# Two inner-layer tiles of a fused attention + MLP kernel handled as one

## The chip, the core and the metric

The kernel runs on one core of a Trainium2 chip. The metric is the time of one execution on the device in microseconds (us); less is better. The engines are TensorE (PE in the profile; PEld is its weight load), VectorE (DVE), ScalarE (ACT), GpSimd (POOL) and the queue that issues the DMAs (SP). Each works through its own instructions in order and waits on semaphores for the others.

## The reference, cut to what matters

```
# attention over clusters: B=4, H=8, S=768, D=64, 16 clusters
mask   = (argmax(q_n @ c_n.T)[:, :, :, None] == argmax(k_n @ c_n.T)[:, :, None, :])
scores = where(mask, (q @ k.T) / sqrt(D), -1e9)
attn   = softmax(scores);  x = (attn @ v) as [3072, 512]
# MLP
h = x @ w_in                    # [3072, 2048]
g = s * relu(h) ** 2 + b
out = g @ w_out                 # [3072, 512]
```

## The kernel before

**Attention in units.** A unit is 128 queries of one head: 4 batches, 3 chunks of 256 tokens each, 4 head pairs, 2 query tiles, 2 heads, so 192 units. A unit takes its scores on TensorE (`scores`, 4 matmuls, L456), the row maximum on VectorE (`maxima`, L465), a tiny bias and the exponential on ScalarE (`exps`, L472 and L475), the f16 high part of the exponential on ScalarE (`high`, L119; on VectorE for some early units) and the low part on GpSimd (`low`, L498), a transposing DMA of both (L500), and the product with V on TensorE (`values`, L517 to L519, two units at a time). After 4 units `finish_x` splits the result into two f16 parts (L540 on ScalarE, L543 on GpSimd) and turns it by DMA into the tiles `x` that the MLP reads.

**MLP in steps.** A step is one chunk of 256 tokens and one of 16 blocks `ft` of 128 inner columns, so 12 chunks of 16 steps, 192 in all. Step by step: `mlp_in` multiplies by 12 matmuls of 128x256 (4 blocks of K, three f16 products each) into a tile `h` in PSUM; `mlp_relu` on ScalarE makes `r` from it (L582), then its square once in f16 as the high part `g[:, 0]` (L584) and once in f32 in place (L585); `mlp_gl` on GpSimd subtracts the one from the other as the low part (L590); `mlp_out` adds 6 matmuls of 128x512 into the two banks of `acc` (L602). After the last step of a chunk, VectorE scales `acc` into `o` (L610) and a DMA stores it. The pool of `h` has one buffer, so the next `mlp_in` waits until L582 has read the last one; `r` has 2 buffers and `g` 4.

**The order.** One loop over `i` writes everything: unit `i`, and MLP step `m = i - LAG` with `LAG = 21`. In turn it writes `scores(i)`, `mlp_out` of step `m-2`, `high(i-1)`, `maxima(i)` and `exps(i)`, `mlp_in` and `mlp_relu` of step `m`, `low(i-1)`, `mlp_gl` of step `m-1`, and in odd `i` `values(i-5)`. Preparations run beside it as generators, one piece in each turn: `prep_q`, and for the next batch `prep_k` and `prep_v`, which start 20 units ahead of it (mostly VectorE), and `wsplit(ft)`, which splits the weights of block `ft`. A scheduler then sets the real order on each engine by a simulation of its own, with what was written first preferred among what is ready; each engine's order is fixed when the kernel runs. A chunk's first step needs all four tiles `x` of its chunk, that is, all 16 of its units.

Of the kernel before, what the change touches and what calls it, by code (L numbers as in the profile page):

```python
# [8 lines left out]
F16 = mybir.dt.float16  # L9
# [9 lines left out]
P = 128  # L19
C = 16  # L20
D = 64
# [5 lines left out]
def tile_cluster_attention_mlp(ctx, tc, q, k, v, cent, w_in, w_out, s_in, b_in, out):  # L27
# [107 lines left out]

    ct = sb.tile([P, 2, D], F32, tag="r", name="ct", bufs=2)
    cn = ct[:, 0, :]
# [14 lines left out]

    cnat = sb.tile([P, 3, 2, D], F16, tag="r", name="cnat", bufs=2)
    G.memset(cnat[:, 1:3], 0.0)
# [402 lines left out]
    def mlp_start(b, c):  # L557
# [9 lines left out]
        MS[(b, c)] = [cf, xm[:, 7:8], None]  # L567

    def mlp_in(b, c, ft):
        n = f"{b}_{c}_{ft}"  # L570
        ph = ps_h.tile([P, 512], F32, tag="h", name=f"h_{n}")
        GS[(b, c, ft)] = ph
        terms = [(kt, wl, xl) for kt in range(KT) for wl, xl in ((0, 0), (0, 1), (1, 0))]
        for i, (kt, wl, xl) in enumerate(terms):
            nc.tensor.matmul(ph[:, :CW], WSP[ft][0][:, wl, kt, :], XS[(b, c, kt)][:, :, xl, :],  # L575
                             start=(i == 0), stop=(i == len(terms) - 1))

    def mlp_relu(b, c, ft):
        n = f"{b}_{c}_{ft}"
        ph = GS[(b, c, ft)]  # L580
        r = sb.tile([P, CW], F32, tag="r", name=f"r_{n}", bufs=2)
        A.activation(r, ph[:, :CW], AF.Relu, scale=MS[(b, c)][0])  # L582
        g = sb.tile([P, 2, CW], F16, tag="g", name=f"g_{n}", bufs=4)
        A.activation(g[:, 0, :], r, AF.Square)  # L584
        A.activation(r, r, AF.Square)  # L585
        GS[(b, c, ft)] = (r, g)

    def mlp_gl(b, c, ft):
        r, g = GS[(b, c, ft)]
        G.tensor_tensor(g[:, 1, :], r, g[:, 0, :], op=ALU.subtract)  # L590
        GS[(b, c, ft)] = g

    def mlp_out(b, c, ft):
        n = f"{b}_{c}"
        if ft == 0:
            MS[(b, c)][2] = ps_a.tile([P, CT, DM], F32, tag="acc", name=f"acc_{n}")
        acc = MS[(b, c)][2]
        g = GS.pop((b, c, ft))
        for t in range(CT):
            rows = slice(t * P, t * P + P)  # L600
            for gl, wl in ((0, 0), (0, 1), (1, 0)):
                nc.tensor.matmul(acc[:, t, :], g[:, gl, rows], WSP[ft][1][:, wl, :],  # L602
                                 start=(ft == 0 and gl + wl == 0), stop=(ft == NF - 1 and gl == 1))
        if ft == NF - 1:
            _, e, acc = MS.pop((b, c))
            o = sb.tile([P, CT, DM], F32, tag="stage", name=f"o_{n}", bufs=3)
            if b + c == 0:
                column_sums()
            for t in range(CT):
                V.scalar_tensor_tensor(o[:, t, :], acc[:, t, :], e, bias[0], op0=ALU.mult, op1=ALU.add)  # L610
            nc.sync.dma_start(out[b * S : (b + 1) * S].rearrange("(p t) e -> p t e", t=T)[:, c * CT : (c + 1) * CT, :], o)
# [7 lines left out]
    def at(step, gen):  # L619
        later.setdefault(step, []).append(gen)  # L620
# [18 lines left out]
    for ft in range(NF):  # L639
        at(LAG - 4 + ft, wsplit(ft))  # L640
    wgen = weights()
# [58 lines left out]
    while i < NU + 8 or i - LAG < NS + 4:  # L700
# [4 lines left out]
        if i < NU:  # L705
            with first_of_all(i):
                scores(i)
        if 0 <= m - 2 < NS:
            mlp_out(*steps[m - 2])
        if 0 <= i - 1 < NU:  # L710
            with first_of_all(i):
                high(i - 1)
        if i < NU:
            with first_of_all(i):
                maxima(i)
                exps(i)
        if 0 <= m < NS:
            if steps[m][2] == 0:
                mlp_start(*steps[m][:2])
            mlp_in(*steps[m])  # L720
            mlp_relu(*steps[m])
        if 0 <= i - 1 < NU:
            with first_of_all(i):
                low(i - 1)
        if 0 <= m - 1 < NS:
            mlp_gl(*steps[m - 1])
# [34 lines left out]
```

## Time and profile before

| | before |
|---|---|
| time, median of 3 runs | 984.87 us (982.25 to 988.37) |
| the profiled execution | 987.78 us |
| its span in the profile | 986.0 us |
| PE / DVE / ACT / POOL busy | 834.3 / 673.0 / 726.4 / 550.2 us |
| `h` matmuls (L575) | 2304, 292.0 us busy |
| `acc` matmuls (L602) | 1152, 295.4 us busy |

The profile is of one execution. A row of a group names the line, engine, operation, the tiles written and read with their shapes, the count, the busy time in us and the mean of one in ns, and then the time its engine sat idle just before, with what ended that. The ends of matmuls are modelled and overlap, so the busy times of single lines on PE add up to more than PE's own.

### The profile page before, as it was taken

What the parts mean: (1) busy time and instruction counts of PE and PEld (TensorE: products, weight loads), DVE (VectorE), ACT (ScalarE), POOL (GpSimd) and SP (SyncE); (2) the same over time, 40 slices, a digit from 0 to 9 for tenths busy, and PEclk for the clock granted to TensorE, in tenths of its full rate; (3) what the DMA queues carried; (4) which work ended last, traced back from release to release, by engine and by line L of the source; (5) the groups of instructions that cost most, each with busy time, mean ns of one, the idle gap of its engine ahead of it and who ended that gap; (6) DMA issues with size and microseconds to landing.
All of it is one profiled execution on the core that took longest, in us unless ns stands there. A gap on an engine that the chain in (4) does not pass through costs nothing. (4 is left out here: it accounts for less than half of the span.)

```text
span 986.0 us, 22497 instructions
## 1 busy us (share of the span) xinstructions
PE 834.3 (85%) x8625; PEld 580.2 (59%) x8625; DVE 673.0 (68%) x1475; ACT 726.4 (74%) x1416; POOL 550.2 (56%) x543
## 2 busy tenths in 40 slices
PE   0568524887899999998799999997889999999997
PEld 0347312654566666765566666765666666767764
DVE  7798889989687665658787756578867567473100
ACT  4476776877578788867678877876788977789443
POOL 3125755556456576655467656655566766667322
PEclk9955566999999999999999999999999999999999
DMA  6865883687678775698888767797888676777200
GB/s 181 204 196 158 222 210 90 138 194 134 128 144 163 156 161 123 140 210 154 171 164 156 169 132 156 138 203 181 138 160 173 151 119 142 142 138 149 44 23 21
DMA packets 450299, 147.36 MB, mean 149 GB/s; under 512 B 417936, under 2 KB 446608, under 8 KB 450192
## 3 DMA queue, kind: packets, MB, share of 16 engines
q1 hardware_dynamic: 450192, 145.93, 69.7%
q8 instruction: 67, 1.10, 0.5%
q14 instruction: 40, 0.33, 0.1%
HBM read 35.69 MB, written 6.29 MB: 43 GB/s over the span
## 5 line engine op out<-in xcount | busy, mean ns | idle before, releaser
L498 POOL TENSOR_TENSOR ph<-p,ph 128x768 f16<-128x768 f32 x184 | 308.6, 1677 | 170.7 <-ACT ph L119 135.8
L575 PE MATMUL h<-x,wis 128*128 128x256 f16 x2304 | 292.0, 275 | 17.3 <-ACT r L582 12.2
L602 PE MATMUL acc<-wos,g 128*128 128x512 f16 x1152 | 295.4, 380 | 4.7 <-POOL g L590 2.9
L575 PEld LDWEIGHTS <-wis 128*128 128x128 f16 x2304 | 223.1, 98 | 74.9 <-issue 16.6
L590 POOL TENSOR_TENSOR g<-r,g 128x256 f16<-128x256 f32 x192 | 133.3, 695 | 139.7 <-ACT r L585 129.8
L465 DVE TENSOR_REDUCE ssm<-sc 128x1 f32<-128x768 f32 x192 | 180.9, 950 | 16.2 <-PE sc L456 16.0
L475 ACT ACTIVATE p<-sc,ssm,qsm 128x768 f32<-128x768 f32 x192 | 188.1, 980 | 3.9 <-DMA PT<-ph 1.8
L602 PEld LDWEIGHTS <-g 128*128 128x128 f16 x1152 | 104.1, 98 | 88.2 <-POOL g L590 6.9
L119 ACT ACTIVATE ph<-p 128x768 f16<-128x768 f32 x174 | 144.8, 832 | 11.1 <-DMA PT<-ph 10.8
L472 ACT ACTIVATE ssm<-ssm,lift,qsm 128x1 f32<-128x1 f32 x192 | 73.4, 382 | 101.9 <-DVE ssm L465 101.4
L517 PE MATMUL px<-vh,PT 128*128 128x65 f16 x1104 | 119.9, 196 | 14.5 <-DVE ksm L98 5.2
L582 ACT ACTIVATE r<-h,cf 128x256 f32<-128x256 f32 x192 | 89.1, 464 | 55.0 <-PE h L575 50.8
L518 PE MATMUL px<-vl,PT 128*128 128x64 f16 x1104 | 119.9, 193 | 0.0
L519 PE MATMUL px<-vh,PT 128*128 128x65 f16 x1104 | 119.9, 194 | 0.0
L456 PE MATMUL sc<-KA,QA 128*128 128x384 f16 x384 | 101.1, 343 | 20.2 <-ACT p L475 16.9
L518 PEld LDWEIGHTS <-PT 128*128 128x128 f16 x1104 | 103.6, 100 | 21.2 <-issue 12.8
L517 PEld LDWEIGHTS <-PT 128*128 128x128 f16 x1104 | 103.9, 98 | 17.5 <-issue 9.1
L456 PE MATMUL sc<-KB,QB 128*128 128x384 f16 x384 | 100.2, 345 | 7.8 <-DMA QB<-qb 7.7
L519 PEld LDWEIGHTS <-PT 128*128 128x128 f16 x1104 | 103.6, 98 | 3.0
L584 ACT ACTIVATE g<-r 128x256 f16<-128x256 f32 x192 | 79.5, 414 | 3.8
L585 ACT ACTIVATE r<-r 128x256 f32<-128x256 f32 x192 | 79.1, 412 | 3.3
L525 DVE TENSOR_SCALAR ssm<-px 128x2 f32<-128x2 f32 x92 | 14.2, 155 | 88.3 <-PE px L519 88.2
(153 smaller groups left out, 1090.9 us busy)
## 6 DMA issues: line engine op xcount, KB each, us to landing
wst<-in_moe_w_in_dram SPq DMA_DIRECT2D x16, 512.0 KB, 4.5
wst<-in_moe_w_out_dram SPq DMA_DIRECT2D x16, 512.0 KB, 4.1
kn<-in_k_dram SPq DMA_DIRECT2D x16, 384.0 KB, 3.9
qn<-in_q_dram SPq DMA_DIRECT2D x24, 256.0 KB, 3.8
vn<-in_v_dram SPq DMA_DIRECT2D x16, 384.0 KB, 4.4
out_dram<-o SPq DMA_DIRECT2D x12, 512.0 KB, 3.2
PT<-ph SPq DMA_TRANSPOSE x184, 3.4
x<-xn SPq DMA_TRANSPOSE x48, 2.5
```

The lines of the kernel that those rows point to most:

```text
L119: A.activation(dst, src, AF.Copy)
L456: last_score[0] = nc.tensor.matmul(sc[:, e, :HALF], X[:, col, :], y[:, h * S + e * HALF : h * S + (e + 1) * HALF], start=st, stop=not st)
L465: last_max[0] = V.tensor_reduce(SM[i // 4][:, 0, j : j + 1], U[i]["sc"], axis=AX.XY, op=ALU.max, negate=True)
L475: last_exp[0] = A.activation(p.rearrange("p (a b) -> p a b", a=2), u["sc"], AF.Exp, bias=bi, scale=u["scale"], **total)
L498: G.tensor_tensor(u["ph"][:, 1, :], u["p"], u["ph"][:, 0, :], op=ALU.subtract)
L517: nc.tensor.matmul(o1, PT[:, kt, :], vh[:, h, kt, : D + 1], start=(kt == 0), stop=False)
L518: nc.tensor.matmul(o, PT[:, kt, :], vl[:, h, kt, :], start=False, stop=False)
L519: nc.tensor.matmul(o1, PT[:, T + kt, :], vh[:, h, kt, : D + 1], start=False, stop=(kt == T - 1))
L575: nc.tensor.matmul(ph[:, :CW], WSP[ft][0][:, wl, kt, :], XS[(b, c, kt)][:, :, xl, :], start=(i == 0), stop=(i == len(terms) - 1))
L582: A.activation(r, ph[:, :CW], AF.Relu, scale=MS[(b, c)][0])
L590: G.tensor_tensor(g[:, 1, :], r, g[:, 0, :], op=ALU.subtract)
L602: nc.tensor.matmul(acc[:, t, :], g[:, gl, rows], WSP[ft][1][:, wl, :], start=(ft == 0 and gl + wl == 0), stop=(ft == NF - 1 and gl == 1))
```

## The change

Two neighbouring steps become one pair. `h` now holds two tiles of 256 columns, one bank of PSUM in all; `r` and `g` are twice as wide and have half the buffers (1 and 2), so they take the same room. Each ScalarE and GpSimd pass goes over both tiles. The numbers of matmuls and their shapes stay. `mlp_in` of a pair is written in the turns with even `m`, its squares in the next turn after the exponential (`mlp_square`, a function of its own now), `mlp_gl` in that turn too, and `mlp_out` three turns after `mlp_in` where it was two. `wsplit` starts one turn sooner. Two small tiles of the prologue, `ct` and `cnat`, get other buffers.

```diff
-    ct = sb.tile([P, 2, D], F32, tag="r", name="ct", bufs=2)
+    ct = sb.tile([P, 2, D], F32, tag="r", name="ct", bufs=1)
-    cnat = sb.tile([P, 3, 2, D], F16, tag="r", name="cnat", bufs=2)
+    cnat = sb.tile([P, 3, 2, D], F16, tag="g", name="cnat", bufs=2)
...
-        ph = ps_h.tile([P, 512], F32, tag="h", name=f"h_{n}")
+        ph = ps_h.tile([P, 2, CW], F32, tag="h", name=f"h_{n}")
-        for i, (kt, wl, xl) in enumerate(terms):
-            nc.tensor.matmul(ph[:, :CW], WSP[ft][0][:, wl, kt, :], XS[(b, c, kt)][:, :, xl, :],
-                             start=(i == 0), stop=(i == len(terms) - 1))
+        for f in range(2):
+            for i, (kt, wl, xl) in enumerate(terms):
+                nc.tensor.matmul(ph[:, f, :], WSP[ft + f][0][:, wl, kt, :], XS[(b, c, kt)][:, :, xl, :],
+                                 start=(i == 0), stop=(i == len(terms) - 1))
...
-        r = sb.tile([P, CW], F32, tag="r", name=f"r_{n}", bufs=2)
-        A.activation(r, ph[:, :CW], AF.Relu, scale=MS[(b, c)][0])
-        g = sb.tile([P, 2, CW], F16, tag="g", name=f"g_{n}", bufs=4)
-        A.activation(g[:, 0, :], r, AF.Square)
+        r = sb.tile([P, 2, CW], F32, tag="r", name=f"r_{n}", bufs=1)
+        A.activation(r, ph, AF.Relu, scale=MS[(b, c)][0])
+        GS[(b, c, ft)] = r
+
+    def mlp_square(b, c, ft):
+        r = GS[(b, c, ft)]
+        g = sb.tile([P, 2, 2, CW], F16, tag="g", name=f"g_{b}_{c}_{ft}", bufs=2)
+        A.activation(g[:, 0], r, AF.Square)
         A.activation(r, r, AF.Square)
...
-        G.tensor_tensor(g[:, 1, :], r, g[:, 0, :], op=ALU.subtract)
+        G.tensor_tensor(g[:, 1], r, g[:, 0], op=ALU.subtract)
...
-        for t in range(CT):
+        for f in range(2):
+            for t in range(CT):
...
-        at(LAG - 4 + ft, wsplit(ft))
+        at(LAG - 5 + ft, wsplit(ft))
...
-        if 0 <= m - 2 < NS:
-            mlp_out(*steps[m - 2])
+        if m % 2 and 0 <= m - 3 < NS:
+            mlp_out(*steps[m - 3])
...
+        if m % 2 and 0 <= m - 1 < NS:
+            mlp_square(*steps[m - 1])
-        if 0 <= m < NS:
+        if m % 2 == 0 and 0 <= m < NS:
             if steps[m][2] == 0:
                 mlp_start(*steps[m][:2])
             mlp_in(*steps[m])
...
-        if 0 <= m - 1 < NS:
+        if m % 2 and 0 <= m - 1 < NS:
             mlp_gl(*steps[m - 1])
```

What the scheduler makes of it is shown at two places. In the names, `h_2_4` is chunk 2, block 4 (the batch is left out), and the last number is that of the buffer's allocation.

On ScalarE, in the middle of chunk 2 of the first batch, before:

```order
L582 ACTIVATE r_2_4_4481<-h_2_4_4468,cf_2_4200 128x256
L584 ACTIVATE g_2_4_4483<-r_2_4_4481 128x256
L119 ACTIVATE ph_4597<-p_4556 128x768
L585 ACTIVATE r_2_4_4481<-r_2_4_4481 128x256
L472 ACTIVATE ssm_4417<-ssm_4417,lift,qsm_0_1_3834 128x1
L475 ACTIVATE p_4601<-sc_4586,ssm_4417,qsm_0_1_3834 128x768
L472 ACTIVATE ssm_4681<-ssm_4681,lift,qsm_0_1_3834 128x1
L582 ACTIVATE r_2_5_4571<-h_2_5_4558,cf_2_4200 128x256
```

And now, the same place after the change (L584 is now the relu, L590 and L591 are the squares):

```order
L584 ACTIVATE r_2_4_4362<-h_2_4_4337,cf_2_4083 128x512
L590 ACTIVATE g_2_4_4441<-r_2_4_4362 128x512
L185 ACTIVATE qb_1_0_4415<-qn_1_0_4197,qsm_1_0_4280 128x4x64 x2
L119 ACTIVATE ph_4435<-p_4335 128x768
L591 ACTIVATE r_2_4_4362<-r_2_4_4362 128x512
L472 ACTIVATE ssm_4307<-ssm_4307,lift,qsm_0_1_3746 128x1
L475 ACTIVATE p_4439<-sc_4418,ssm_4307,qsm_0_1_3746 128x768
L119 ACTIVATE ph_4459<-p_4439 128x768
L472 ACTIVATE ssm_4307<-ssm_4307,lift,qsm_0_1_3746 128x1
L475 ACTIVATE p_4463<-sc_4454,ssm_4307,qsm_0_1_3746 128x768
L584 ACTIVATE r_2_6_4490<-h_2_6_4465,cf_2_4083 128x512
```

From one relu to the next there lay one exponential (L475) before, and two now; three passes serve two steps where six did.

On GpSimd, where chunk 1 ends and chunk 2 begins in the second batch (the preparation of the third batch is about over there), before:

```order
L590 TENSOR_TENSOR g_1_14_7612<-r_1_14_7610,g_1_14_7612 128x256
L498 TENSOR_TENSOR ph_7673<-p_7595,ph_7673 128x768
L590 TENSOR_TENSOR g_1_15_7695<-r_1_15_7693,g_1_15_7695 128x256
L498 TENSOR_TENSOR ph_7743<-p_7678,ph_7743 128x768
L498 TENSOR_TENSOR ph_7840<-p_7747,ph_7840 128x768
L590 TENSOR_TENSOR g_2_0_7772<-r_2_0_7770,g_2_0_7772 128x256
```

And now (L596 is the subtraction for the pair):

```order
L596 TENSOR_TENSOR g_1_14_7416<-r_1_14_7344,g_1_14_7416 128x512
L543 TENSOR_TENSOR xn_7134<-xs_6971,xn_7134 128x2x128
L498 TENSOR_TENSOR ph_7180<-p_7159,ph_7180 128x768
L498 TENSOR_TENSOR ph_7288<-p_7184,ph_7288 128x768
L375 COPY qa_0_1_7267<-qb_0_1_7268 128x8x64
L428 MEMSET vh_0_9726 128x12x2
L498 TENSOR_TENSOR ph_7313<-p_7292,ph_7313 128x768
L543 TENSOR_TENSOR xn_7389<-xs_7255,xn_7389 128x2x128
L498 TENSOR_TENSOR ph_7409<-p_7317,ph_7409 128x768
L498 TENSOR_TENSOR ph_7458<-p_7414,ph_7458 128x768
L498 TENSOR_TENSOR ph_7569<-p_7462,ph_7569 128x768
L596 TENSOR_TENSOR g_2_0_7575<-r_2_0_7497,g_2_0_7575 128x512
```

The low parts of units (L498) between the last pair of chunk 1 and the first of chunk 2 are 6 now; between two pairs elsewhere there are mostly 2. Before, there were 3 for the two steps from `g_1_14` to `g_2_0`. So in the stretch before this place the MLP stands up to 4 steps further ahead of the units than it did, and here 4 more units pass without an MLP step. The same happens at this place in the first and the third batch.

More of the change, by code (lines that the diff above doesn't have):

```diff
@@ L598, in mlp_out @@
         g = GS.pop((b, c, ft))
-        for t in range(CT):
[L600 to L604, printed above, removed]
+        for f in range(2):
+            for t in range(CT):
+                rows = slice(t * P, t * P + P)
+                for gl, wl in ((0, 0), (0, 1), (1, 0)):
+                    nc.tensor.matmul(acc[:, t, :], g[:, gl, f, rows], WSP[ft + f][1][:, wl, :],
+                                     start=(ft + f == 0 and gl + wl == 0), stop=(ft + f == NF - 1 and gl == 1))
+        if ft == NF - 2:
             _, e, acc = MS.pop((b, c))
```

## The prediction

> **What bounds the kernel now.** I read the page's first two parts, then the windows of 50 us, the waits of TensorE and the chain that ended last. First the page: busy time of the engines, and the 40 slices of PE with its granted clock.
>
> ```profile
> PE 834.3 (85%) x8625; PEld 580.2 (59%) x8625; DVE 673.0 (68%) x1475; ACT 726.4 (74%) x1416; POOL 550.2 (56%) x543
> PE   0568524887899999998799999997889999999997
> PEclk9955566999999999999999999999999999999999
> ```
>
> The 85% is an average over two stages: PE is patchy for a quarter of the span, at a lower clock, and at 9 tenths or more after that, with two dents. The windows show the stages (start and end, length, then busy us and instructions of PE, PEld, DVE, ACT and POOL, granted clock, DMA share, GB/s):
>
> ```profile
> 150.00:200.00 50.00, 34.72 (x397) 24.00 (x397) 46.40 (x107) 38.21 (x73) 28.97 (x23) 0.80 0.47 106
> 200.00:250.00 50.00, 39.10 (x386) 24.73 (x384) 45.54 (x96) 37.56 (x70) 30.05 (x25) 0.95 0.82 165
> 400.00:450.00 50.00, 47.08 (x535) 33.39 (x533) 31.51 (x75) 38.87 (x78) 29.35 (x28) 1.00 0.83 175
> 450.00:500.00 50.00, 42.50 (x474) 29.61 (x470) 39.66 (x100) 37.42 (x71) 27.36 (x28) 1.00 0.81 165
> 500.00:550.00 50.00, 47.24 (x556) 33.41 (x555) 39.31 (x83) 40.64 (x78) 32.16 (x32) 1.00 0.88 171
> 650.00:700.00 50.00, 42.88 (x487) 30.48 (x485) 41.89 (x100) 36.50 (x71) 27.60 (x27) 1.00 0.82 171
> 750.00:800.00 50.00, 49.34 (x545) 34.48 (x543) 31.63 (x74) 40.91 (x81) 31.40 (x30) 1.00 0.73 156
> ```
>
> Up to 250 us VectorE is the full engine (46.40 and 45.54 of 50). From then on TensorE is: 47 to 49 of 50, but only 42.50 and 42.88 where the next batch is prepared and VectorE has 40 to 42 of 50. ScalarE, which the change relieves most, never has over 41. The chain that ended last has TensorE's work end to end in such a stretch (start, us, group):
>
> ```profile
> 618.56 1.29 PE acc L602 x6
> 619.86 1.30 PE sc L456 x8
> 621.15 1.31 PE h L575 x12
> ```
>
> So a step costs PE 1.31 + 1.29 = 2.60 us, and a unit 1.30 / 2 = 0.65 for its scores and, by this group's row, 119.9 / 1104 x 6 = 0.65 for its product with V: 1.30 in all, and 3.90 for a unit and a step.
>
> ```profile
> L517 PE MATMUL px<-vh,PT 128*128 128x65 f16 x1104 | 119.9, 196 | 14.5 <-DVE ksm L98 5.2 <-DVE xs L529 4.6 <-DVE xm L98 3.9
> ```
>
> The change keeps all this work. It can win only what PE stands idle, and from 250 us to the end its waits say for whom (us in total, times, longest):
>
> ```profile
> PE h L575 <- ACT r L582: 12.2, 10, 3.1
> PE sc L456 <- ACT p L475: 6.0, 6, 1.8
> PE sc L456 <- DMA QB<-qb: 5.8, 7, 2.0
> PE px L517 <- DVE ksm L98: 3.7, 3, 1.7
> PE acc L602 <- POOL g L590: 2.4, 6, 0.6
> ```
>
> **The passes themselves: nothing directly.** The groups, with equal shapes together:
>
> ```profile
> L582 ACT ACTIVATE r<-h,cf 128x256 f32<-128x256 f32 x192 | 89.1, 464 | 55.0 <-PE h L575 50.8 <-DVE xm L565 1.9 <-POOL g L590 0.8
> L584 ACT ACTIVATE g<-r 128x256 f16<-128x256 f32 x192 | 79.5, 414 | 3.8
> L585 ACT ACTIVATE r<-r 128x256 f32<-128x256 f32 x192 | 79.1, 412 | 3.3
> L119 ACT ACTIVATE ph<-p 128x768 f16<-128x768 f32 x174 | 144.8, 832 | 11.1 <-DMA PT<-ph 10.8 <-POOL ph L498 0.2
> L475 ACT ACTIVATE p<-sc,ssm,qsm 128x768 f32<-128x768 f32 x192 | 188.1, 980 | 3.9 <-DMA PT<-ph 1.8 <-POOL ph L498 0.8
> L472 ACT ACTIVATE ssm<-ssm,lift,qsm 128x1 f32<-128x1 f32 x192 | 73.4, 382 | 101.9 <-DVE ssm L465 101.4
> L267 ACT ACTIVATE wos<-wo,glob 128x512 f16<-128x512 f32 x16 | 11.5, 718 | 7.3 <-DVE wis L269 5.7 <-DVE glob L258 1.5
> L498 POOL TENSOR_TENSOR ph<-p,ph 128x768 f16<-128x768 f32 x184 | 308.6, 1677 | 170.7 <-ACT ph L119 135.8 <-ACT p L475 6.7 <-DVE ph L121 6.3
> L590 POOL TENSOR_TENSOR g<-r,g 128x256 f16<-128x256 f32 x192 | 133.3, 695 | 139.7 <-ACT r L585 129.8 <-DMA PT<-ph 4.5 <-issue 3.8
> L223 POOL TENSOR_TENSOR wi<-wi,wsg 128x512 f32<-128x512 f32 x16 | 20.1, 1255 | 33.1 <-PE pw L221 16.9 <-ACT ssm L472 13.5 <-DVE xs L529 2.7
> ```
>
> ScalarE: from 256 to 768 elements a pass grows by (832 - 414) / 512 = 0.816 ns an element, so a square over 512 takes 414 + 209 = 623 ns and a relu 464 + 209 = 673 (a scaled pass of 512 takes 718: the upper bound). 192 x (464 + 414 + 412) = 247.7 us become 96 x (673 + 2 x 623) = 184: 63 us less. GpSimd: (1677 - 695) / 512 = 1.92 ns, so 1186 for 512 (1255 at most): 133.3 become 114 to 120. Both lie beside PE's work; alone they are worth nothing, and count only through waits.
>
> **The wait for `h`: -5.1 us.** `mlp_in` needs the one bank of `h` read. Now PE has the next `mlp_out` and a unit between two `mlp_in` (1.29 + 1.30 = 2.6 us of cover for a pass of 0.46); then an `mlp_out` of a pair and two units (2.58 + 2.60 = 5.2 for 0.67). It takes a ScalarE that is over 4 us late, and the longest wait now is 3.1. But where the 12.2 us lie matters:
>
> ```profile
> PE h L575 <- ACT r L582: 3.0, 1, 3.0
> PE h L575 <- ACT r L582: 4.1, 2, 3.1
> ```
>
> These are the waits within 450 to 500 and 650 to 700: 7.1 us in the dents. There PE waits for a slow attention whatever name the wait bears. I count 12.2 - 7.1 = 5.1 as gone (bounds 0 and 12.2).
>
> The Trainium skill, Perfetto Trace Analysis, section Matmuls, says that independent groups of matmuls should rotate through PSUM banks, so that one is emptied beside the next one's matmuls. It speaks against a pair in one bank. By it each pair would stop PE for its relu, 96 x 0.67 = 64 us more; the wait row speaks for the cover, since one bank served 192 tiles with 10 waits.
>
> **The second product a turn later: -1.8 us.** `acc<-g` waits 2.4 us now; a turn of 3.9 us more before it removes them, apart from the last one (start, us, group, idle before):
>
> ```profile
> 980.07 1.04 PE L602 MATMUL acc<-wos,g 128*128 128x512 f16 x4 [0.60 <-POOL g L590]
> ```
>
> At the end the last `mlp_in` is followed by the second product before it (1.29) and two matmuls of the last (0.43), then this 0.60: 2.32 from `h` to `g`, of which the passes are 0.46 + 0.41 + 0.41 + 0.70 = 1.98 and hops 0.34. The pair's passes take 0.67 + 0.62 + 0.62 + 1.19 + 0.34 = 3.44 against 2.58 + 0.43: 0.43 of wait. The tail stays as it is.
>
> **ScalarE earlier for the exponentials: -2 us.** `sc <- p` is 6.0 us; 63 us less in its queue lets exponentials come sooner, but passes half as long again can stand in front of one. I take a third (0 to 6).
>
> **One buffer of `r`.** The next relu waits for GpSimd to be done with the last pair. Squares and subtraction are written a turn before, 3.9 us for 1.19, or 1.19 + 1.68 with a unit's low part ahead. That hides it: 0. Where it doesn't, the next unit's bias and exponential queue behind the relu, and GpSimd's low part, the transposing DMA and PE's `values` wait for those; ScalarE at 41 of 50 has room for about 1.5 us a pair before PE feels it.
>
> **The prologue's buffers: 0.** Other free buffers for `ct` and `cnat`. `wsplit` a turn sooner moves the same VectorE passes by one turn in a stage where VectorE is full anyway; I take 0 within 2 us either way.
>
> **The change of batch: -3.5 us, the term I know least.** By the order, the MLP gets up to 4 steps further ahead of the units where the next batch is prepared, and then 4 units pass without a step. The gain: 4 x 2.60 = 10.4 us of PE work move into a stretch in which PE idles 50 - 42.50 + 50 - 47.24 = 10.3 us. What comes back: in 4 units alone PE has 1.30 us of work each, and the pace is between ScalarE's 0.98 + 0.83 + 0.38 = 2.19 us and today's pace outside the dents, 50 / 13 = 3.85 (exponentials in a window, busy us and count):
>
> ```profile
> 450.00:500.00 50.00, 9.78 (x10) 1.00 0.81 165
> 800.00:850.00 50.00, 12.78 (x13) 1.00 0.65 135
> ```
>
> That is 4 x 0.89 = 3.6 to 4 x 2.55 = 10.2 of new idle. I take 8 absorbed and 6.8 given back (a pace of 3.0, between the ends, as VectorE still has preparation to do): 1.2 a change, 3.5 for three. The ends are 3 x (10.3 - 3.6) = 20 gained and, if nothing is absorbed, 3 x 10.2 = 31 lost.
>
> **The sum.** 5.1 + 1.8 + 2 + 3.5 = 12.4, so a span of 986.0 - 12.4 = 973.6. The profiled execution took 987.78, 1.8 more than its span, and lies 2.9 above the median of 984.87; against that median the change gives 972.5, and I say **973**.
>
> **The rivals.**
> - *The waits only change their names.* In the dents the attention sets the pace (10 units in 50 us against 13), the order is fixed, and what PE no longer waits for `h` it waits for scores or `px`. Only the 1.8 and a few us remain: 975 to 992, likeliest 982. For it: no engine but PE is full after 250 us, and most of the `h` waits lie in the dents.
> - *The starved boundary (slower).* At the first step of chunk 2 the MLP has nothing to do until all 16 units of its chunk are through, PE has 1.30 us a unit, and the steps run ahead have not filled the dent, since PE's waits there were for scores behind which the steps queue. Price 3 x 10.2 less the 8.9 of the other terms: +22, 1006; with half absorbed +6, 991. It decides from a pace where what is given back is over what is absorbed, 1.30 + 8 / 4 = 3.3 us a unit; against it speaks that ScalarE needs 2.19.
> - *The dents close.* All 10.3 us absorbed and the units alone at 2.19 us: 20 + 8.9 = 29 less, 956.
> - *A lower clock at the boundaries.* At 150 to 200 us, PE 70% busy, the granted clock is 0.80. If 4 lonely units of 1.30 us ran so, it would cost 3 x 5.2 x 0.25 = 4 us: 977. Against it stands the longest wait for `h`, in a window of clock 1.00:
>
> ```profile
> 475.18 1.47 PE L575 MATMUL h<-x,wis 128*128 128x256 f16 x12 [3.05 <-ACT r L582]
> ```
>
> The Trainium skill, TensorE: Matmul & The Clock Gate, Part 1, has the clock halve after an idle window of about 3.4 us; no wait that long is in the rows above, so this trace neither shows nor denies it.
> - *The bank blocks.* If the relu stopped PE in each pair, 985 + 64 = 1049; 10 waits in 192 speak against it.
>
> **How the numbers follow.** The forecast (966 to 975) has 0.40, the closed dents 0.08, the renamed waits 0.31, the clock 0.04, the starved boundary 0.15, the bank 0.02. About 1% (9.8 us) is what a measurement here tells from no change: faster 0.40 + 0.08 = 0.48, within 0.31 + 0.04 = 0.35, slower 0.15 + 0.02 = 0.17. The range of 959 to 993 leaves out the bank, most of the starved boundary and the lowest part of the closed dents, and takes in the bounds of the smaller terms.
>
> **What the profile after would show.** Right: ScalarE near 663 us and GpSimd near 533, relu near 0.67 us, `h <- r` below 5 us, no `acc <- g` but at the end, PE's busy time within 1%. Wrong, and how: a PE window below 40 of 50 at the start of a chunk 2 (the starved boundary); waits of the relu for GpSimd above a few us (the one buffer of `r`); `sc` or `px` waits grown by what `h` lost (renamed waits). The prediction fails if the attention's own pace, not PE, sets the time between 400 and 750 us.

## The result: 1.6% slower, and the profile after

| | before | after |
|---|---|---|
| time, median of 4 runs | 985.79 us (982.25 to 988.37) | 1001.46 us (998.58 to 1004.51) |
| ratio, with its 95% interval | | 1.0156 (1.0121 to 1.0191) |
| the profiled execution; its span | 987.78; 986.0 us | 999.52; 997.8 us |
| mean granted clock of TensorE | 0.941 | 0.921 |

The prediction said 973 us, 959 to 993; the time lies above its range. The page of after (busy times, then TensorE's busy share and its granted clock in 40 slices of 25 us):

```profile
PE 844.6 (85%) x8625; PEld 589.1 (59%) x8625; DVE 681.1 (68%) x1475; ACT 688.9 (69%) x1128; POOL 532.6 (53%) x447
...
PE   1567425987899699999899799998996999999997
...
PEclk9966656998999799999799999998999999999999
```

ScalarE and GpSimd did get their relief (726.4 to 688.9 and 550.2 to 532.6 us). TensorE ran the same 8625 matmuls but was busy 10.3 us longer, and its clock row now has sevens far behind the start, where the row of before has none. The three merged passes came out as costed:

```profile
L596 POOL TENSOR_TENSOR g<-r,g 128x512 f16<-128x512 f32 x96 | 115.3, 1201 | 115.2 <-ACT r L591 103.8
...
L584 ACT ACTIVATE r<-h,cf 128x512 f32<-128x512 f32 x96 | 65.1, 678 | 62.0 <-PE h L577 56.2
...
L590 ACT ACTIVATE g<-r 128x512 f16<-128x512 f32 x96 | 60.0, 625 | 1.9
```

TensorE's waits from 250 us on (us in total, times, longest):

```profile
PE sc L456 <- ACT p L475: 10.8, 7, 2.3
PE h L577 <- DMA x<-xn: 10.3, 7, 3.3
...
PE h L577 <- ACT r L584: 3.3, 6, 0.8
...
PE acc L609 <- POOL g L596: 0.4, 1, 0.4
```

The wait of `h` for the relu fell from 12.2 to 3.3 us and that of `acc` from 2.4 to 0.4: what the change was to take away, it took away. In their place TensorE waits 10.3 us for the tiles `x` of a chunk and 10.8 for ScalarE to free a score bank (6.0 before).

Both rows below belong to stretches in which a batch is prepared (columns as in the windows of before):

```profile
200.00:250.00 50.00, 40.53 (x375) 24.66 (x373) 44.83 (x85) 34.05 (x56) 23.45 (x17) 0.90 0.67 148
...
450.00:500.00 50.00, 42.88 (x435) 29.64 (x434) 40.28 (x95) 31.27 (x50) 22.99 (x19) 0.90 0.83 177
```

TensorE's busy time there is about what it was (39.10 and 42.50 before), but fewer matmuls fit into the second one (435 for 474), at a clock of 0.90 for 1.00. Windows of 2 us around 480 us show why. TensorE is at the first pair of the second batch there (TensorE's busy time and matmuls, granted clock, DMA share, GB/s):

```profile
476.00:478.00 2.00, 1.04 (x6) 1.00 0.06 14
478.00:480.00 2.00, 0.07 (x3) 0.76 1.14 300
480.00:482.00 2.00, 1.93 (x21) 0.50 1.06 269
482.00:484.00 2.00, 0.21 (x2) 0.50 0.88 157
484.00:486.00 2.00, 2.00 (x11) 0.50 0.94 241
486.00:488.00 2.00, 2.00 (x26) 0.50 1.29 276
488.00:490.00 2.00, 2.00 (x30) 0.68 1.10 92
```

and the timeline there (start, us, group, and the idle time before it):

```profile
479.96 0.17 PE L388 MATMUL pq<-cT,QA 128*128 128x16 f16 x1 [1.93 <-DVE vm L98]
...
483.79 3.36 PE L577 MATMUL h<-x,wis 128*128 128x256 f16 x15 [1.86 <-DMA x<-xn]
...
488.92 2.95 PE L577 MATMUL h<-x,wis 128*128 128x256 f16 x24
```

From 476 to 480 us TensorE works 1.11 us of 4. The clock falls to 0.50 at 479 us and stays there to 489, and 15 matmuls of `h` take 3.36 us where 24 take 2.95 behind it. A wait for `x` falls into the slow stretch.

The Trainium skill, TensorE: Matmul & The Clock Gate, Part 1, has the clock at half after an idle window of about 3.4 us, with a window that runs free of the program. The trace agrees on the half and on the window: the clock falls at 479.03 us and rises at 489.27, three times 3.41 us later. It doesn't agree that the window has to be idle. These are that stretch of after in windows of 3.41 us, counted from the fall:

```profile
475.62:479.03 3.41, 1.44 (x8) 1.00 0.51 113
479.03:482.44 3.41, 1.98 (x21) 0.50 1.08 284
482.44:485.86 3.42, 2.07 (x10) 0.50 0.86 188
485.86:489.27 3.41, 3.41 (x45) 0.50 1.35 205
489.27:492.68 3.41, 3.41 (x41) 1.00 0.61 154
```

The fall follows a window with 1.44 us of work, in which no wait had yet lasted longer than about 1 us. The longest single wait of before (3.05 us, in the prediction) left the clock alone. On the grid of that trace's own clock changes it lies across two windows, and each of them has more work:

```profile
470.58:473.99 3.41, 1.55 (x18) 1.00 1.49 207
473.99:477.41 3.42, 2.23 (x34) 1.00 0.82 248
```

So the work within one such window tells here what the length of a wait doesn't. The 20 traces of this case bear it out: all their clock changes lie on such a grid, all 176 windows at full clock with less than 1.49 us of work (from 5 us on) were followed by the half clock, and none with more than 2.28 us was; between the two figures both happen.

**Where the time went.** From windows of 10 us between 180 us and the end, TensorE's busy time splits into work (busy x clock) and clock loss (busy x (1 - clock)); the rest is idle:

| from 180 us on | span | work | clock loss | idle |
|---|---|---|---|---|
| before | 986.0 | 742.7 | 4.6 | 58.7 |
| after | 997.8 | 736.9 | 20.4 | 60.5 |

Of the 11.8 us of span, 15.8 stand as clock loss, 1.8 as idle time, and the work reads 5.8 less. TensorE idles as long as before: the waits that the change took away came back under other names. But the idle time now lets the clock fall 10 times between 180 us and the end of the work, where it fell 3 times in before. That is where the time shows; whether the clock is the cause is another matter, taken up with the extra matmuls.

**What changed in the order.** Counted on TensorE, when an MLP step starts, `scores` stands 21.5 to 26 units ahead of it from step 4 on in before, as long as there are units. In after the lead of a pair falls to between 18 and 20 in steps 24 to 32, 74 to 80 and 120 to 128: the steps run ahead of the units, as the prediction had read from the order. Then the first pair of a chunk 2 (steps 32, 80 and 128) stands on TensorE with its `x` not made:

```profile
332.10 0.68 PE L577 MATMUL h<-x,wis 128*128 128x256 f16 x3 [3.31 <-DMA x<-xn]
```

The stretch around 480 us is not of this kind: its pair is step 64, with a lead of 22 in both kernels.

### The profile page after: what moved, and what is told of

The parts are those of the page before. It is cut to its first block, busy times and chain, and to the rows that moved or that the text cites. A ratio compares the mean times of both kernels' runs of the same rounds, so it can differ in the third digit from the quotient of the medians.

```text
span 997.8 us, 22110 instructions
## 1 busy us (share of the span) xinstructions
PE 844.6 (85%) x8625; PEld 589.1 (59%) x8625; DVE 681.1 (68%) x1475; ACT 688.9 (69%) x1128; POOL 532.6 (53%) x447
## 4 chain that ended last, share of the span: by engine, by line
PE 49%; DVE 8%; DMA 6%; issue 2%; POOL 2%; ACT 1%; SPq 1%; POOLq 0%; DVEq 0%; ACTq 0%
PE h L577 18%; PE acc L609 17%; PE sc L456 6%; PE px L517 2%; PE px L519 2%; PE px L518 2%; DVE ssm L465 2%; POOL ph L498 1%; DVE oe_q L291 1%; DMA kn<-in_k_dram 1%; DMA QA<-qa 1%; DMA PT<-ph 1%; DMA x<-xn 1%; DMA QB<-qb 1%; DVE oo_q L293 1%
## 5 line engine op out<-in xcount | busy, mean ns | idle before, releaser
L498 POOL TENSOR_TENSOR ph<-p,ph 128x768 f16<-128x768 f32 x184 | 309.4, 1682 | 203.7 <-ACT ph L119 159.8
L577 PE MATMUL h<-x,wis 128*128 128x256 f16 x2304 | 289.6, 280 | 19.7 <-DMA x<-xn 10.3
L609 PE MATMUL acc<-wos,g 128*128 128x512 f16 x1152 | 273.8, 381 | 0.8 <-POOL g L596 0.7
L577 PEld LDWEIGHTS <-wis 128*128 128x128 f16 x2304 | 227.0, 100 | 67.8 <-issue 17.5
L475 ACT ACTIVATE p<-sc,ssm,qsm 128x768 f32<-128x768 f32 x192 | 188.2, 980 | 9.4 <-DMA QB<-qb 1.7
L609 PEld LDWEIGHTS <-g 128*128 128x128 f16 x1152 | 110.2, 98 | 115.5 <-POOL g L596 2.9
L596 POOL TENSOR_TENSOR g<-r,g 128x512 f16<-128x512 f32 x96 | 115.3, 1201 | 115.2 <-ACT r L591 103.8
L517 PE MATMUL px<-vh,PT 128*128 128x65 f16 x1104 | 117.7, 199 | 11.1 <-DVE xs L529 4.5
L519 PE MATMUL px<-vh,PT 128*128 128x65 f16 x1104 | 117.2, 197 | 0.0
L517 PEld LDWEIGHTS <-PT 128*128 128x128 f16 x1104 | 105.6, 100 | 14.0 <-issue 8.1
L518 PEld LDWEIGHTS <-PT 128*128 128x128 f16 x1104 | 105.1, 102 | 12.8 <-issue 8.0
L584 ACT ACTIVATE r<-h,cf 128x512 f32<-128x512 f32 x96 | 65.1, 678 | 62.0 <-PE h L577 56.2
L456 PE MATMUL sc<-KB,QB 128*128 128x384 f16 x384 | 103.4, 351 | 4.0 <-DMA QB<-qb 4.0
L519 PEld LDWEIGHTS <-PT 128*128 128x128 f16 x1104 | 105.4, 100 | 0.0
L456 PEld LDWEIGHTS <-QA 128*128 128x128 f16 x384 | 36.1, 102 | 48.7 <-issue 26.9
L590 ACT ACTIVATE g<-r 128x512 f16<-128x512 f32 x96 | 60.0, 625 | 1.9
```

The source lines that it names most:

```text
L456: last_score[0] = nc.tensor.matmul(sc[:, e, :HALF], X[:, col, :], y[:, h * S + e * HALF : h * S + (e + 1) * HALF], start=st, stop=not st)
L475: last_exp[0] = A.activation(p.rearrange("p (a b) -> p a b", a=2), u["sc"], AF.Exp, bias=bi, scale=u["scale"], **total)
L498: G.tensor_tensor(u["ph"][:, 1, :], u["p"], u["ph"][:, 0, :], op=ALU.subtract)
L517: nc.tensor.matmul(o1, PT[:, kt, :], vh[:, h, kt, : D + 1], start=(kt == 0), stop=False)
L518: nc.tensor.matmul(o, PT[:, kt, :], vl[:, h, kt, :], start=False, stop=False)
L519: nc.tensor.matmul(o1, PT[:, T + kt, :], vh[:, h, kt, : D + 1], start=False, stop=(kt == T - 1))
```

## The experiments

Ratios are to the kernel before on the same chip, with 95% intervals. One thing holds for all of them: with each edit the scheduler plans the whole order anew. TensorE's order in `hold` leaves that of after at 157 us, and `holdhalves` leaves that of `hold` at 185 us. So a run tells what an edit costs together with the order that was planned for it; no run here holds the order fixed and changes the passes alone. Only `holdws` has the order of another run, `hold`, from start to end.

### The order alone

`hold` is the changed kernel with one line more: `mlp_in` of step `m` must not stand ahead of the scores of its unit on TensorE. `hold23` also has the MLP two units later.

```
-            mlp_in(*steps[m])
+            with behind(last_score[0]):
+                mlp_in(*steps[m])
```

> The changed kernel with one rule more for the scheduler: mlp_in of step m may not stand on TensorE ahead of the scores of unit m + 21, so the MLP cannot run ahead of the units. All passes stay wide. Order theory (the loss is the stretch of 4 units without MLP work at the start of a chunk 2, and the TensorE clock of 0.5 that follows it): no TensorE window of 10 us from 180 us on with a granted clock under 0.9, clock loss (busy time x (1 - clock)) from 180 us on near the 4.6 us of before instead of 20.4, waits of h for x under 3 us instead of 10.3; time 973 to 987. Width theory (the passes of 512 make the exponentials late, wherever the MLP stands): order alone changes little, 996 to 1004.

> The same with LAG = 23 instead of 21: two units more between a unit and its MLP step, so a chunk's x has about 7.8 us more to arrive. Order theory: where waits of h for x or thin stretches are left in the run with 21, they go; time equal to that run or up to 6 us below it. If the lead does not matter: the same within 3 us, or slower by the two extra steps at the end if the tail were not full (it is at 9 tenths now, so at most 1 to 2 us).

Measured: `hold` 1.0037 (1.0010 to 1.0063), `hold23` 1.0084 (1.0053 to 1.0115). In `hold` the lead is 22 or more in every pair as long as there are units, and 1.2 of the 1.6% are gone: with wide passes the run-ahead, and what else the order had with it, cost some 12 us. But neither expectation of `hold` came out. The kernel doesn't come below before, its clock loss stays at 18.1 us, and `h` still waits 5.7 us for `x`. So removing the run-ahead doesn't remove the thin stretches. More lead on top of it made the kernel 0.5% slower; the part behind the last exponential, where MLP steps alone are left, is 4.2 us longer in its profile (72.5 for 68.3).

### The width of the passes

`holdhalves` is `hold` with each pass of 512 as two of 256 (the rule of the hold, the shared bank and the second product's turn stay; the rest of the order is planned anew); `halves` is the same without the hold; `holdact` splits ScalarE's three passes alone.

```
-        A.activation(r, ph, AF.Relu, scale=MS[(b, c)][0])
+        for f in range(2):
+            A.activation(r[:, f], ph[:, f], AF.Relu, scale=MS[(b, c)][0])
```

> The held order, but each pass of ScalarE and GpSimd over a pair is two passes of 256 again (relu, both squares, subtraction); pairs, banks and the second product stay. ScalarE back to about 726 us and GpSimd to 550. Order theory: within 1% of the held kernel with wide passes (975 to 992), as ScalarE was never the bound. Width theory: faster than the held kernel with wide passes by several us.

> The changed kernel without the held order, its passes split in two of 256 each. The scheduler here lets the MLP run ahead as far (the lead of the units falls from 22 to 16 in the first batch, to 20 in the next two). Order theory: slow like the changed kernel, 995 to 1010, with windows of clock near 0.5 after the thin stretch, most of it in the first batch. Width theory: back to 984 to 990 although the order is the bad one.

> The held order, relu and squares as two passes of 256 each again, GpSimd's subtraction one pass over 512. Held with all passes wide was 1.0037 of before, with all narrow 0.9975. If ScalarE's long passes and its wait for both tiles cost the 6 us: 0.995 to 0.999. If GpSimd's long pass does (one buffer of r, freed late): 1.002 to 1.005.

Measured: `holdhalves` 0.9975 (0.9954 to 0.9995), `halves` 1.0018 (0.9998 to 1.0038), `holdact` 1.0020 (1.0005 to 1.0035). Kernels with narrow passes are faster, by 1.4% without the hold (1.0156 to 1.0018) and by 0.6% with it (1.0037 to 0.9975). The four together:

| | wide | narrow |
|---|---|---|
| steps may run ahead | 1.0156 | 1.0018 |
| held | 1.0037 | 0.9975 |

The two parts don't add up. The hold is worth 1.2% with wide passes and 0.4% with narrow ones, though in `halves` the lead falls further in the first batch (to 16.5) than in after. Either remedy alone takes most of the loss away, so the loss can't be shared out between them. The order theory of `halves` (slow like the changed kernel) did not come out.

`holdact` lies 0.45% above `holdhalves`, so GpSimd's pass of 1.2 us has a part, as the second half of its expectation has it; its 0.17% below `hold` lie within the intervals, so a part of ScalarE's passes is not shown. ScalarE is busier in `holdhalves` (706.5 us) than in `hold` (689.4), and the kernel is faster.

### The weights' split a turn later

`holdws` puts `wsplit` back to where it was.

```
-        at(LAG - 5 + ft, wsplit(ft))
+        at(LAG - 4 + ft, wsplit(ft))
```

> The changed kernel with the held order, and wsplit at its old turn (LAG - 4). In the trace of the held kernel all of its loss against before lies ahead of step 32, in the stage where weights are split. If the earlier wsplit does it (VectorE's weight passes in front of the attention's), this gets back to 982 to 989; if not, within 3 us of the held kernel's 1.004 of before.

Measured: 1.0070 (1.0045 to 1.0094), no better than `hold`. In the two traces all four engines run the same instructions in the same order, so in the held kernel the turn changes nothing and can't be what costs; without the hold it was not tried. The 0.3% between the two ratios, taken on two chips, is what two measurements of one order can differ by here. Smaller differences between the runs below are not to be read.

### Without the preparation of later batches

`before_keep`, `after_keep`, `halves_keep` and `hold_keep` leave out `prep_k` and `prep_v` for batches 1 to 3 and use batch 0's K and V again.

```
-            for hp in range(NP):
-                at(48 * b - 20 + 4 * hp, prep_k(b, hp))
-            at(48 * b - 20, prep_v(b))
+            at(48 * b - 20, keep(b))
```

> The kernel before, without the preparation of K and V for batches 1 to 3: they reuse those of batch 0 (this is left out, so only the time counts). The stretches in which VectorE prepares a batch go. Both theories: TensorE dense from about 260 us on, clock 1.00, about 25 to 45 us below the kernel before (945 to 962).

> The changed kernel with the same left out; here the scheduler lets the MLP run ahead of the units nowhere (22 to 23 units of lead). If the loss of the change comes from the stretches where a batch is prepared (run ahead, thin TensorE, low clock), it goes with them: this kernel 3 to 12 us faster than the one before with the same left out, clock loss from 180 us on within 3 us of it. If wide passes cost time wherever they stand: 5 to 15 us slower than it, with clock 1.00.

> The changed kernel with narrow passes and without the preparation of K and V for batches 1 to 3 (batch 0's are used again). With wide passes that kernel gave 0.9324 against the kernel before and 0.9865 against the kernel before with the same left out. Theory A (where TensorE sets the pace a pass's width is worth nothing either way): 0.929 to 0.937. Rival B (wide passes hold the buffers longer): under 0.928. Rival C (the saved passes are what won there): above 0.939, near the 0.9458 of the kernel before with the same left out.

> The held order without the preparation of K and V for batches 1 to 3 (batch 0's are used again). Without the hold this gave 0.9324. Theory A (the order costs only where the preparation starves TensorE): 0.929 to 0.936. Rival B (holding costs by itself): above 0.938; if the run-ahead cost everywhere: under 0.928.

| | whole | without preparation | price of three preparations |
|---|---|---|---|
| before | 1 | 0.9458 (0.9420 to 0.9495) | 5.4% |
| changed | 1.0156 | 0.9324 (0.9299 to 0.9350) | 8.3% |
| changed, held | 1.0037 | 0.9347 (0.9316 to 0.9377) | 6.9% |
| changed, narrow | 1.0018 | 0.9387 (0.9355 to 0.9419) | 6.3% |

This is the answer to where the gain went. Where no later batch is prepared, the change is 1.4% faster than before (920.92 against 933.48 us), and narrow passes are no gain there (0.7% slower than wide ones). The order can't be judged by these runs: without the preparation the scheduler lets the MLP run ahead nowhere (22 or more units of lead in `after_keep` too), so the hold had nothing to do. The preparations then take back 8.3 - 5.4 = 2.9%, some 28 us. Some expectations missed: `before_keep` came out below its range (945 to 962), `after_keep` is 12.6 us faster than it where 3 to 12 were expected, and `halves_keep` lies between A and C. The page of `after_keep` has no thin slice and no low clock behind the start:

```profile
PE   0567433798999999999999999999999999999997
...
PEclk9975655799999999999999999999999999999999
```

### Which preparation, and the weights' split

Where the 28 us lie can be read from the same profiles, one execution each: the time in us from the exponential of unit 28 to that of unit 60, and so on for the other two changes of batch, whole, without the preparation, and the difference.

| | units 28 to 60 | 76 to 108 | 124 to 156 |
|---|---|---|---|
| before | 159.5 - 137.0 = 22.5 | 143.0 - 129.2 = 13.8 | 143.1 - 128.5 = 14.6 |
| changed | 170.1 - 137.8 = 32.3 | 150.1 - 124.7 = 25.4 | 146.2 - 124.7 = 21.5 |
| changed, held | 169.4 - 139.7 = 29.7 | 146.9 - 124.7 = 22.2 | 147.2 - 124.7 = 22.5 |

The changed kernel pays more at each of the three changes, by 10, 12 and 7 us (such a stretch can differ by some 4 us between two executions of one order, as `firstwide` shows below). What the first one has besides is the split of the weights.

The stretch from the exponential of unit 28 to that of unit 60 is the first change of batch; `wsplit` runs into it, with a ScalarE and a VectorE pass for each of 32 tiles, of which 13 fall into this stretch in `hold`. One window for each kernel (its second number is the length of the stretch; the number behind the busy times is the clock): before, after, `hold`, `holdhalves`.

```profile
199.72:359.24 159.52, 142.51 (x1481) 95.61 (x1479) 125.21 (x264) 119.44 (x227) 91.72 (x84) 0.97 0.78 154
```

```profile
204.53:374.67 170.14, 146.81 (x1458) 98.15 (x1459) 124.16 (x260) 110.22 (x179) 86.20 (x68) 0.92 0.70 143
```

```profile
204.84:374.22 169.38, 144.90 (x1470) 96.97 (x1471) 125.18 (x264) 111.75 (x180) 89.88 (x69) 0.92 0.72 144
```

```profile
204.19:364.87 160.68, 142.06 (x1464) 95.53 (x1462) 124.98 (x261) 113.80 (x226) 89.01 (x84) 0.95 0.69 150
```

In these profiles the two kernels with wide passes take 9 to 10 us longer here with the same 124 to 125 us of VectorE's work; at the other two changes `hold` and `holdhalves` differ by 2 and 4 us, in opposite directions. But part of it is chance: `firstwide` (below) runs in the order of `hold`, with its passes, up to 11 us before the end of this stretch, and took 165.4 us. And `hold23` and `holdsoon`, wide and held with other orders, took 160.3 and 160.8. `before_ns` and `hold_ns` leave most of the split out, in before and in `hold`; four split pieces stand in for the rest:

```
+        if ft > 3:
+            WSP[ft] = WSP[ft % 4]
+            return
```

> The kernel before without the split of weight pieces 4 to 23: the first four split pieces stand in for them. This takes 40 ScalarE and 40 VectorE passes out of units 20 to 40. Control for hold_ns. If the split crowds the first change (theory A), units 28 to 60 fall from 159.5 to 140 to 152 us, ratio 0.980 to 0.993; if K's and V's preparation alone fills it (rival B), to no less than 155 us, ratio 0.994 to 1.000.

> The same left out of the changed kernel in the held order (wide passes). Theory A (wide passes cost 9 us at the first change because they stand in ScalarE's and GpSimd's queues ahead of the weights' split, on which the first steps wait): units 28 to 60 come within 3 us of before_ns, and the ratio to before_ns falls to 0.990 to 0.998. Rival B (wide passes cost there because they delay the preparation of K and V, split or not): 7 to 10 us longer than before_ns between units 28 and 60, ratio to before_ns 1.002 to 1.008. Rival C (the loss is the order's still): as B, but with low granted clock at both later changes too.

The counts in these two texts are wrong: there are 16 pieces, so 12 were left out, and 24 passes on each of the two engines.

Measured: `before_ns` 1.0018 (0.9999 to 1.0037), `hold_ns` 0.9902 (0.9870 to 0.9934). Without the split the wide kernel gains 1.35% on `hold`. The 20 units ahead of the stretch take 109.4 us for 114.9, and the stretch falls to

```profile
199.10:359.12 160.02, 140.97 (x1493) 96.24 (x1492) 118.01 (x246) 102.44 (x165) 85.87 (x69) 0.97 0.74 153
```

with the clock back at 0.97. Before gains nothing: its stretch takes 156.6 us for 159.5 and its ratio lies at the edge of what rival B had for it (0.994 to 1.000). The stretch of `hold_ns` comes within 3.4 us of that, and `hold_ns` takes 0.9902 / 1.0018 = 0.988 of `before_ns`, a little beyond theory A on the good side and much like the 0.986 without preparation. So the split costs the held kernel with wide passes what it doesn't cost before, each with its own order. Why is not shown: `hold23` has wide passes and 16 tiles of the split in this stretch and is as short as before there (0.8 us longer), so the two together don't lengthen it in every order.

`mix`, `firstnarrow` and `firstwide` ask the same in the times: `hold` with narrow passes around all three changes (96 steps, with 96 wide ones, not 54 as its text says), in steps 0 to 35 alone, and everywhere but there.

```
+    def cut(b, c, ft):
+        m = (b * NCH + c) * NF + ft
+        return (0, 1) if m < 36 else (slice(0, 2),)
...
+        for f in cut(b, c, ft):
+            A.activation(r[:, f], ph[:, f], AF.Relu, scale=MS[(b, c)][0])
```

> The held order with narrow passes (384 becomes two of 256, three of them on ScalarE and one on GpSimd) for the steps below 36, from 54 to 83 and from 102 to 131, that is around the changes of batch, and the wide passes in the other 54 or so of 192 steps. Narrow passes everywhere gave 0.9975, wide ones everywhere 1.0037. Theory A (the width of a pass costs only where TensorE runs thin, at the changes of batch): 0.990 to 0.9985, as fast as narrow everywhere or faster, clock loss 11 to 15 us. Rival B (the width costs everywhere, as a longer hold of r and of the bank of h): half way, 0.999 to 1.002.

> The held order with narrow passes in steps 0 to 35 alone, wide ones in the 156 steps behind. Theory A (wide passes cost at the first change alone, beside the split of the weights): units 28 to 60 in 159 to 163 us, ratio 0.990 to 0.998, no slower than narrow passes everywhere (0.9975). Rival B (they cost everywhere a little): 1.001 to 1.004.

> The held order with wide passes in steps 0 to 35 alone, narrow ones behind. Theory A: units 28 to 60 in 166 to 172 us, ratio 1.003 to 1.009. Rival B: 0.998 to 1.001.

| steps 0 to 35 | wide behind | narrow behind |
|---|---|---|
| wide | `hold` 1.0037 | `firstwide` 1.0016 (0.9992 to 1.0041) |
| narrow | `firstnarrow` 0.9986 (0.9965 to 1.0007) | `holdhalves` 0.9975 |

Narrow passes in the first 36 steps bring 0.4 to 0.5%, in the other 156 they bring 0.1 to 0.2%, which is within the intervals. Both expectations of `firstnarrow` and `firstwide` missed by a little: the cost leans to the first change, as theory A has it, but the stretch alone (162.7 and 165.4 us in their profiles) carries less than the 9 us that the profiles of `hold` and `holdhalves` gave it. `mix` came out at 0.9990 (0.9970 to 1.0010), too close to both ranges, with a clock loss of 16.9 us where theory A had 11 to 15.

### Extra matmuls against the low clock

`holdwarm` and `before_warm` lay two extra matmuls of 128x384 ahead of the scores in 36 units around the changes; the real scores overwrite them.

```
+        if 30 < i < 160 and ((i + 12) % 48 < 5 or i > 47 and i % 48 < 7):
+            y = KA.rearrange("p n q -> p (n q)")
+            for e in range(2):
+                nc.tensor.matmul(sc[:, e, :HALF], QA[:, col, :], y[:, h * S + e * HALF : h * S + (e + 1) * HALF], start=True, stop=True)
```

> The changed kernel with the held order, and in 36 units around the changes of batch two extra matmuls of 128x384 into the score bank just ahead of the real scores, which overwrite them: they compute nothing, and keep TensorE from running thin. The held order alone gave a ratio of 1.0037 with 18.1 us of clock loss behind 180 us (before: 4.6). Theory A (the thin stretches cost twice, since the granted clock falls to 0.50 for several us behind them): the clock loss falls to under 9 us, the 72 extra matmuls cost at most 72 x 0.163 = 11.7 us, mostly laid into idle time, and the ratio lies between 0.993 and 1.006, no more than 0.3% above the same matmuls in the kernel before. Rival B (the work that is ready decides, the clock only follows): the clock loss stays at 15 to 18 us and the ratio rises to 1.008 to 1.016.

> The kernel before with the same extra matmuls: what they cost where the clock loss is 4.6 us already. Both theories: a ratio of 1.002 to 1.012 (nothing hidden: 11.7 us, 1.0118; nine tenths hidden: 1.001).

Measured: `holdwarm` 1.0146 (1.0094 to 1.0197), `before_warm` 0.9962 (0.9947 to 0.9977). In `holdwarm` the clock loss stays at 18.7 us and the ratio rises by 1.1%, near the whole price of the extra work (11.7 us of 991): rival B. In before the same matmuls cost nothing, the kernel is even 0.4% faster, which no theory here had. Its profile has 13 us less idle time behind 180 us and 9 us more work, at the same clock loss; its order, too, is another from 235 us on, and whether that is what won is not known. As a test of the clock this falls short: an extra matmul that waits with the scores for the same bank can't run while TensorE waits for that bank, for `x` or for VectorE. Of one kernel's own runs, those at a lower clock are the longer ones (28 runs of before beside `hold`: clocks of 0.933 to 0.945, spans of 982.1 to 991.1 us, correlation -0.83), but that doesn't say which makes which.

### The second product's turn alone

`holdsoon` is `hold` with the second product at the earlier turn.

```
-        if m % 2 and 0 <= m - 3 < NS:
-            mlp_out(*steps[m - 3])
+        if m % 2 == 0 and 0 <= m - 2 < NS:
+            mlp_out(*steps[m - 2])
```

> The changed kernel in the held order with the second product of steps m and m+1 at turn m+2, as early as the kernel before has it, and not at m+3. The prediction priced the later turn at 1.8 us, the waits of the second product for the subtraction. Theory A (that price holds): waits of acc for g rise from under 2 us to 2 to 12 us in all, ratio 1.004 to 1.013. Rival B (the later turn costs, since it holds two buffers of g a unit longer): ratio under 1.002.

Measured: 1.0129 (1.0095 to 1.0163), so the later turn, with the order that goes with it, is worth 0.9% with wide passes. TensorE's waits from 250 us on:

```profile
PE px L517 <- DVE xm L98: 8.1, 8, 1.9
PE px L517 <- DVE oe_q L289: 7.2, 3, 3.3
...
PE acc L609 <- ACT g L590: 3.9, 4, 1.1
...
PE acc L609 <- POOL g L596: 2.3, 3, 0.9
```

The wait for `g` is 6.2 us, with 2.2 in `hold`, as theory A had it; 5.9 us more show in the waits of `px` (5.2 and 4.2 us for the same two in `hold`).

## Why the prediction was wrong, point by point

- **The passes** (0): right in the durations, 0.68, 0.63 and 1.20 us for 0.67, 0.62 and 1.19. ScalarE's busy time fell by 37.5 us and not by 63: the rows of the three passes do come to 63 us less, but ScalarE's rows overlap (all of them add up to 813 us in before, where it is busy for 726), and some of the overlap goes with the passes. "Nothing directly" counted only their busy time; the kernels with passes of this length are 0.6% slower in the held order and 1.4% without the hold, each with the order planned for it.
- **The wait of `h` for the relu** (-5.1): right in sign, -8.9 in the waits. The shared bank blocked next to nothing (3.3 us left, in 6 waits).
- **The second product** (-1.8): the wait fell by 2.0. Undoing the turn costs 9 us, so the term looks too small once the passes are wide, as far as the order of `holdsoon`, planned anew, lets one say.
- **The exponentials** (-2): wrong; `sc <- p` grew from 6.0 to 10.8 us.
- **The prologue and `wsplit`** (0 within 2): the turn of `wsplit` changes nothing in the held kernel, where turning it back gave the same order. That the split was safe in a stretch "where VectorE is full anyway" did not hold: leaving it out wins 1.35% in the held kernel and nothing in before.
- **The change of batch** (-3.5, bounds -20 and +31): this is the step that failed. The three preparations cost the changed kernel 2.9%, or 28 us, more than the kernel before, next to the bad end; the rest of the kernel gained (0.9458 - 0.9324) x 985.8 = 13 us, where the other terms had 8.9. The one less the other is the loss of 0.0156 x 985.8 = 15 us. The term took 8 us of each dent as filled by the steps run ahead, and 6.8 as lost behind it. TensorE's busy time in the windows of 50 us says otherwise. In the second batch 450 to 550 us has 1.1 us more than before and 550 to 600 us 3.3 less; in the third 650 to 750 us has 6.0 more and 750 to 800 us 7.3 less; and the clock loss comes on top.

  The rival of the starved boundary named this part: steps run ahead, don't fill the dent, and then TensorE stands at the first step of chunk 2 for `x`. It had 0.15, and its time with nothing absorbed (1006) was near the 1001 measured. That is partly luck, since the run-ahead is not the whole loss: the rival had neither the width of the passes, nor the split, nor the clock. Its sign missed by a little: the lowest windows at such a start are near 42 of 50, not below 40, the first of them at a low clock as well:

```profile
300.00:350.00 50.00, 42.11 (x462) 29.57 (x461) 31.80 (x75) 30.00 (x48) 25.84 (x22) 0.86 0.65 128
...
750.00:800.00 50.00, 42.08 (x475) 29.79 (x473) 34.02 (x76) 36.77 (x61) 31.26 (x25) 0.97 0.72 144
```

- **The renamed waits** (a rival of 0.31 at 975 to 992): right for the idle time, which is 60.5 us for 58.7; the loss that it didn't have stands as clock loss. TensorE's busy time rose by 1.2% with it, where the prediction had it within 1%.
- **The clock** (a rival of 0.04 at +4 us): its sign was right and its size was not. 15.8 us more of clock loss stand in the trace, but they come with the thin stretches; that a kept-up clock would win them back was not shown.

Settled: the change wins where no batch is prepared and loses more at all three changes. Holding the order alone takes away 1.2% of the 1.6%, narrow passes alone 1.4%, both 1.8%. Open: how much of the width's cost is the passes and how much the order that the scheduler plans for them, by which queue the first change becomes longer (the waits there are spread over many pairs), how much of the lost time the clock itself makes, and why the extra matmuls don't cost the kernel before anything.

No version that computes everything beat before clearly: `before_warm` (0.9962) and `holdhalves` (0.9975) come lowest.

## What to carry to other kernels

Price a change of an order by stage, and first of all in the stretches where the program does something else besides: there a kernel can lose more than it wins elsewhere, and a merged pass that saves busy time can still come with a slower kernel. When a wait goes, a scheduler uses the room; see in the order who is now ahead of whom, and try a rule that holds the lead where a buffer of work must last through a dent. Where a scheduler plans the order, compare the orders of two runs before reading their difference as that of the edit. Leaving a whole stage out of both kernels is a cheap experiment that tells at once in which stage a gain was lost.

## What the hardware showed

- The granted clock falls to 0.50 in a kernel whose TensorE is 85% busy, without a long wait: 1.44 us of work in a window of 3.41 us were too few, with no wait over about 1 us in that window, and the clock came back three such windows later, behind one that was full.
- An idle time of 3.05 us in one piece didn't lower it in the kernel before, where it lay across two windows with 1.55 and 2.23 us of work.
- Leaving out 24 ScalarE and 24 VectorE passes of the weights' split, beside which VectorE has 125 of 160 to 170 us of work, won nothing in the kernel before and 1.35% in the changed one with the held order.
